# The first expert rows through a second DMA queue, and their squares on VectorE

## The chip, the cores and the metric

The kernel runs on one core of a Trainium2 chip. The core has five engines with programs of their own: TensorE multiplies matrices (PE in the profile, its weight loads are PEld), VectorE (DVE) and ScalarE (ACT) work on rows, GpSimd (POOL) does elementwise work beside them, and SyncE (SP) here only issues transfers. They meet through semaphores. The metric is the device time of one launch in microseconds; lower is better. The kernel before takes 1449.18 us (median of three runs, 1448.63 to 1451.13).

## The reference

For 2048 tokens of 576 features the result is `g * a + (1 - g) * b`, row by row:

```python
g = _sigmoid((x * gate_w).sum(-1, keepdims=True))
# a: a long convolution of each feature over time (state space model), by FFT, plus u * Dskip
# b: experts picked by product keys
q = jnp.einsum("nd,dhc->nhc", xf, w_q)               # 32 heads, two halves of 128
s1, s2 = scores of the halves against k1, k2          # 64 keys each
# best 2 of each, best 2 of the 4 sums, softmax -> gates g, expert numbers top_e
act = _gelu(jnp.einsum("nd,nhkd->nhk", xf, u[top_e]))
out = jnp.einsum("nhk,nhk,nhkd->nd", g, act, v[top_e])
```

The inputs that this change speaks of are the tokens `x` (the same array as the input of the convolution) and the expert rows `u`, 4096 rows of 576 features.

## The kernel before

The kernel does not gather the picked experts. It computes the products of all 2048 tokens with all 4096 expert rows (tile `a`), puts the gates at the picked places with one-hot products (tile `S`), and multiplies the resulting 2048 x 4096 weights with all rows of `v` (tile `o`). The scores are products of the folded query weights with the tokens (tile `s`). The convolution runs as matrix products in between. All large products are of 16-bit halves: a 32-bit operand is scaled by a power of two and split into a high and a low f16 part, and three products (high-high, high-low, low-high) are added up.

The power of two comes from the data. `scale_first` (line 500) does this for the two operands that are wanted first, the first 512 tokens and the first 512 expert rows: each is loaded as two halves of 256 features (tiles `xs` and `us`, 128 partitions by 2 by 512) and a rest of 64 features (`xr` and `ur`, stored twice, on both halves of the partitions); ScalarE squares the pieces and adds the squares of each partition into a column of `sc`; TensorE adds the columns over the partitions with a matrix of ones (tile `sq`); VectorE makes the scale from the sum (`root_scale`, line 346). Then the operand is split: for the tokens VectorE does both parts in `x_first` (line 478), for the expert rows ScalarE takes the high part and VectorE the low part in `u_build` (line 1323). The result tiles are `xb` and `uhl`, with `wrem` for the 64 features of the rest of the expert rows. The squares of the tokens are written into the tile `xb` of the next 512 tokens, and `x_norm` (line 460) multiplies them with ones on TensorE to get the norm of each token: for the first tokens it first runs eight such products whose result is overwritten, then waits until the expert scale is written, then runs the five that count.

The order of work is written by a planner inside the kernel's build. Pieces of work are Python generators; `clock` is TensorE's own time as the planner reckons it, each engine has a planned end time, and a generator that yields is taken up again when the planned clock has come so far. `dma` (line 200) issues a transfer and reckons with one wire and one queue when it lands. `ready(x)` yields until a tile is planned to be there. `marks` are lists by which the generators tell each other how far they are. The engines then run their programs strictly in the order in which the instructions were written; the planner's times decide only that order.

Transfers are issued on SyncE's queue, in the order of the program: the rest and the halves of the first tokens (`x_load`, line 430), the rest and the halves of the first expert rows (`u_load`, line 1309), the keys `kt`, the second 512 tokens, the query weights (`w_load`, line 565), the constants. The one use of ScalarE's queue is for half of the very last output rows (line 1628). The opening of the program is lines 1648 to 1655 for the transfers and 1687 to 1695 for the generators; lines 1703 to 1719 write the first 56 products `a`, in the order in which the split pieces come ready.

Of the kernel before, what the change touches and what calls it, by code (L numbers as in the profile page):

```python
# [17 lines left out]
AF = mybir.ActivationFunctionType  # L18
OP = mybir.AluOpType
# [119 lines left out]
def body(ctx: ExitStack, tc: tile.TileContext, xT, au, par, logdt, dskip, gatew, wq, kT, uT, vv,  # L139
         cst_d, tu_d, tk_d, tf_d, out):  # L140
    nc = tc.nc
# [3 lines left out]
    clock = [0.0]  # L145
    heap = []
    nseq = [0]
    rdy = {}
    table = [None]
    banks = set()  # L150
    wire = [0.0]
    queue = [0.0]
    tiling = [None]

    columns = set()
# [1 line left out]
    def key(x):  # L157
        n = x.tensor.name
        return (n, x.offset) if n in columns else n

    def size(x):
        n = 1
        for d in x.shape[1:]:
            n *= d
        return n
# [30 lines left out]
    S = Engine(nc.scalar, rdy, clock, key, act_cost)  # L196
    V = Engine(nc.vector, rdy, clock, key, dve_cost)
    G = Engine(nc.gpsimd, rdy, clock, key, lambda op, o, a, k: 0.15 + 0.0021 * size(o))

    def dma(o, i, q=None):  # L200
        t = max(clock[0], rdy.get(key(i), 0.0), queue[0])
        queue[0] = t + 0.45
        wire[0] = max(wire[0], t) + (2 if o.dtype in (F16, BF16) else 4) * o.shape[0] * size(o) / 3.4e5
        rdy[key(o)] = max(rdy.get(key(o), 0.0), wire[0] + 2.2)
        (q or DQ).dma_start(o, i)

    def mm(o, l, r, start, stop, cost=None):
        m = l.shape[0] > 64, 128 if size(l) > 64 else size(l)
        if m != tiling[0]:
            tiling[0] = m  # L210
            clock[0] += 0.13 if m == (True, 128) else 0.1
        clock[0] += (size(r) * (4 if r.dtype == F32 else 1) / 2400 + 0.003) if cost is None else cost
        rdy[key(o)] = clock[0] + 0.4
        T.matmul(o, l, r, start=start, stop=stop)  # L214
# [20 lines left out]
    def ready(*xs, late=0.0):  # L235
        while True:
            t = max(rdy.get(key(x), 0.0) for x in xs) + late - clock[0]
            if t <= 0:
                return
            yield t  # L240
# [20 lines left out]
    def need(tag, n=1):  # L261
        while True:
            lst = sorted(slots[tag])
            if len(lst) >= n and lst[n - 1] <= clock[0]:
                return
            yield max(0.2, lst[n - 1] - clock[0]) if len(lst) >= n else 0.3
# [6 lines left out]
    def free(tag, *outs):  # L273
        if owed[tag]:
            owed[tag] -= 1
            return
        slots[tag].append(max([clock[0]] + [rdy.get(key(x), 0.0) for x in outs]))
# [12 lines left out]
    def bank(tag, name):  # L290
        take(tag, name)
        t = ps.tile([128, 512], F32, tag="ps", name=name, bufs=8)
        banks.add(t.tensor.name)
        return t
# [7 lines left out]
    def row(x, name, pool):  # L302
        t = pool.tile([128, D], F32, name=name)
        dma(t, bass.AP(tensor=x.tensor, offset=x.offset, ap=[[0, 128], [1, D]]))
        return t
# [7 lines left out]
    def au_load(a, t):  # L313
        for d, o in au_rows(au, t, a):
            dma(o, d)
# [15 lines left out]
    sc = cp.tile([128, 192], F32, name="sc")  # L331
# [4 lines left out]
    def newcol(again=False):  # L336

        col[again] += 1
        c = 96 + col[1] % 96 if again else col[0]
        return slice(c, c + 1)  # L340

    def short(c0, n):

        return sc[:, c0:c0 + n].bitcast(BF16)[:, 1:2 * n:2]

    def root_scale(bound2, margin, again=False):

        c, h, a, b = (newcol(again) for _ in range(4))
        V.tensor_scalar(sc[:, c], bound2, margin, 2.0 ** -120, op0=OP.mult, op1=OP.max)
        V.tensor_scalar(sci[:, h], sc[:, c].bitcast(I32), 24, 23, op0=OP.logical_shift_right, op1=OP.logical_shift_left)  # L350
        V.tensor_scalar(sci[:, a], sci[:, h], -1.0, float(204 << 23), op0=OP.mult, op1=OP.add)
        V.tensor_scalar(sci[:, b], sci[:, h], float(50 << 23), None, op0=OP.add)
        return sci[:, a].bitcast(F32), sci[:, b].bitcast(F32)
# [32 lines left out]
    def slot(shape, dt, name):  # L386
        take("slot", name)
        return bp.tile([128] + shape, dt, tag="s", name=name, bufs=9)
# [32 lines left out]
    idx = wj.tile([128, NT, 64, 2], F16, name="idx")  # L421
    xb = []

    def halves_load(a, src, c):

        columns.add(a.tensor.name)
        for m in (0, 2):
            dma(a[:, m:m + 2], src[128 * m:128 * m + 256, c].rearrange("(k p) n -> p k n", p=128))

    def x_load(tb):  # L430
        a = slot([4, 512], F32, f"xs{tb}")
        r = pl.tile([128, 512], F32, tag="xr", name=f"xr{tb}", bufs=2)
        c = slice(512 * tb, 512 * tb + 512)
        if tb > 0:
            dma(a, xT[0:512, c].rearrange("(k p) n -> p k n", p=128))
        dma(r[0:64], xT[512:576, c])
        dma(r[64:128], xT[512:576, c])
        if tb == 0:
            halves_load(a, xT, c)
        return a, r  # L440

    def squares(a, r, sq, dst):
# [10 lines left out]
        V.tensor_reduce(out=dst, in_=p[:, 0:2], axis=AX, op=OP.add)  # L453
        free(tag, dst)

    marks = {"x": [], "s": [], "h": [], "u": []}
    first_u = [None, None]
    ahead, normed = [], []

# [18 lines left out]
    def x_first():  # L478

        a, r = xl.pop(0)  # L480
        b = slot([9, 512], F16, "xb0")
        first_u[1] = b
        ahead.append(slot([9, 512], F16, "xb1"))
        sq = ahead[0][:, 0:5].bitcast(BF16)
        s, i = yield from scale_first(a, r, sq)
        spawn(x_norm(0, sq))
        V.tensor_copy(i_x[:, 0:1], i)
        for k in range(5):
            while k == 2 and not marks["s"]:
                yield 0.1  # L490
            o, lo, src = (b[:, k], b[:, 4 + k], a[:, k, :]) if k < 4 else (b[:, 8], b[64:128, 8], r)
            p = slice(0, 128) if k < 4 else slice(64, 128)
            V.tensor_scalar(o, src, s, None, op0=OP.mult)
            V.scalar_tensor_tensor(lo, src[p], s[p], o[p], op0=OP.mult, op1=OP.subtract)
            marks["x"].append(V.free + 0.28)
        scaled.append(0)
        free("slot", b)
        xb.append(b)

    def scale_first(a, r, sq, keep=None):  # L500

        acc = [newcol() for _ in range(3)]
        yield from ready(r)
        S.activation(sq[:, 4], r, AF.Square, accum_out=sc[:, acc[0]])
        for n, m in enumerate((0, 2)):
            yield from ready(a[:, m:m + 2])
            S.activation(sq[:, m:m + 2], a[:, m:m + 2], AF.Square, accum_out=sc[:, acc[n + 1]])
        yield from ready(sq)
        yield from need("kb")
        p = bank("kb", "sq")  # L510
        for n in range(3):
            mm(p[:, 0:1], onesb, short(acc[n].start, 1), n == 0, n == 2, 0.05)
        yield from ready(p)
        out = root_scale(p[:, 0:1], 1.02)
        if keep is not None:
            V.tensor_copy(keep, p[:, 0:1])
        free("kb", out[0])
        return out

    def x_build(tb):  # L520
        while tb - 1 not in scaled:
            yield 0.3
        if tb not in xl:
            yield from need("slot", 2)
            xl[tb] = x_load(tb)
# [783 lines left out]
    def u_load(c):  # L1309
        a = slot([4, 512], F32, f"us{c}")  # L1310
        r = actp.tile([128, 512], F32, tag="ur", name=f"ur{c}")
        cs = slice(512 * c, 512 * c + 512)
        if c:
            dma(a, uT[0:512, cs].rearrange("(k p) n -> p k n", p=128))
        dma(r[0:64], uT[512:576, cs])
        dma(r[64:128], uT[512:576, cs])
        if c == 0:
            halves_load(a, uT, cs)
        return a, r

    uhl, i_u = {}, {}
# [1 line left out]
    def u_build(c):  # L1323
        while adone[0] < c - (kdone[0] < NCK or sdone[0] >= 7):
            yield 0.3
        if c:
            yield from need("raw")
            take("raw", "raw")
            yield from need("slot")
        a, r = xl.pop("u") if c == 0 else u_load(c)  # L1330
        if c:
            yield from ready(a, r)
# [3 lines left out]
        if c == 0:  # L1336
            first_u[0] = hl
            s, i = yield from scale_first(a, r, sq, nu[:, 0:1])
            marks["s"].append(1)
        else:  # L1340
            yield from squares(a, r, sq, nu[:, c:c + 1])
            s, i = root_scale(nu[:, c:c + 1], 1.02)
# [289 lines left out]
    def finish(t, po):  # L1632
# [7 lines left out]
        for d, o in au_rows(out, t, a):  # L1640
# [5 lines left out]
    acts = [(c, tb, j) for c, tb in [(c, tb) for c in range(7) for tb in range(4 if c < 6 else 2)] + [(7, 0), (7, 3), (6, 2), (6, 3), (7, 1), (7, 2)]  # L1646
            for j in range(4)]
    xl = {0: x_load(0)}
    take("raw", "raw")
    xl["u"] = u_load(0)  # L1650
    dma(kt, kT)
    xl[1] = x_load(1)
    w_load(0, 0)
    w_load(0, 1)
# [55 lines left out]
    for w, n in ((0, 9), (1, 5)):  # L1710
        for xk in [x for k in range(4) for x in (k, 4 + k)[:2 - w]] + [8]:
            k = 4 if xk == 8 else xk % 4
            landed("x", k)
            landed("hu"[w], k)
            for j in range(4):
                cs = slice(128 * j, 128 * j + 128)
# [8 lines left out]
    while groups or acts:  # L1725
# [5 lines left out]
        if groups and bank_free() and lag < (6.0 if not a_ok else 2.0 if not turn_s else 5.0 if kdone[0] < NCK else 8.0):  # L1731
            c, t = groups[0]
# [9 lines left out]
        if acts and bank_free():  # L1742
            c, tb, j = acts[0]
# [31 lines left out]
    for t in ORDER:  # L1775
        until(lambda: t in st)
        h = st.pop(t)
# [70 lines left out]
```

## Time and profile before

| what | us |
|---|---|
| median of 3 runs | 1449.18 (1448.63 to 1451.13) |
| profiled execution, from first to last instruction (its span) | 1447.6 |
| TensorE busy | 1426.9 |
| VectorE busy | 1208.5 |
| ScalarE busy | 769.6 |
| GpSimd busy | 481.5 |
| first ones-product of the long run on TensorE | at 9.37 |
| first product `a` | at 15.06 |

The profiled execution has no time of its own beside its span; the median of the runs is 1.6 us above it. A row of the timeline gives the start, the length, the engine, the line, the operation, the written tile, the tiles read and the shapes; in brackets is how long the engine sat idle before it and for what. Nearly all instructions carry the line of a helper (134 for VectorE, ScalarE and GpSimd, 205 for transfers, 214 for matrix products), so they are told apart by their tiles. A window's row gives busy time by engine, with the number of instructions in brackets, then the granted TensorE clock as a share of the full one, the busy share of the 16 DMA engines, and GB/s.

### The profile page before, as it was taken

The page shows a single profiled execution, that of the slowest core. Times are in us where ns is not written, and L with a number is a line of the kernel's source. Part 1 is how long each engine was busy: PE and PEld are TensorE (multiplying, and loading weights), DVE is VectorE, ACT ScalarE, POOL GpSimd, SP SyncE. Part 2 cuts the span into 40 slices and gives each one's busy share as a digit, 9 for nine tenths or more (in the row PEclk, how much of TensorE's full clock was granted, in tenths as well). Part 3 has the DMA queues.
Part 4 walks back from the last instruction along what each step waited for, and adds up shares of the span by engine and source line. Part 5 has one row for each costly group of instructions (what it writes and reads, how often), then busy time and mean ns, then how long its engine had stood idle before and what let it go on. Part 6 is the DMA issues. An engine that isn't in the chain of part 4 may idle for free.

```text
span 1447.6 us, 36680 instructions
## 1 busy us (share of the span) xinstructions
PE 1426.9 (99%) x14105; PEld 852.3 (59%) x14105; DVE 1208.5 (83%) x4598; ACT 769.6 (53%) x1285; POOL 481.5 (33%) x491
## 2 busy tenths in 40 slices
PE   7999999999999999999999999999999999999998
PEld 3444445455455445445555444456887887888787
DVE  6899899889877997885899897589999988888850
ACT  6346876796684776844656655655434223323310
POOL 0325357547356436220547899600000000000000
PEclk9999999999999999999999999999999999999999
DMA  8235323342324333169675777776543333342400
GB/s 308 74 117 159 96 74 120 125 143 72 117 93 150 95 105 99 49 199 293 209 272 179 255 256 270 267 259 210 196 127 111 108 120 107 123 145 68 157 10 17
DMA packets 134351, 215.42 MB, mean 149 GB/s; under 512 B 10912, under 2 KB 79904, under 8 KB 127776
## 3 DMA queue, kind: packets, MB, share of 16 engines
q1 hardware_dynamic: 134080, 213.01, 45.5%
q8 instruction: 110, 1.80, 0.5%
q14 instruction: 65, 0.53, 0.1%
q10 hardware_dynamic: 96, 0.07, 0.0%
HBM read 141.74 MB, written 71.30 MB: 147 GB/s over the span
## 4 chain that ended last, share of the span: by engine, by line
PE 89%; DMA 2%; DVE 2%; issue 0%; ACT 0%; SPq 0%; ACTq 0%; DVEq 0%
PE o L214 26%; PE s L214 24%; PE a L214 23%; PE S L214 4%; PE kb L214 2%; PE pr L214 2%; PE wb L214 2%; PE y L214 1%; PE kP L214 1%; PE pv L214 1%; PE u L214 1%; PE k L214 1%; DMA z_d<-vo 1%; DMA ksb<-k_d 1%; DVE i L134 1%; DMA vn<-in_au_dram 0%
## 5 line engine op out<-in xcount | busy, mean ns | idle before, releaser
L214 PE MATMUL o<-vhl,wh 128*128 128x288 f16 x3072 | 387.0, 286 | 0.0
L214 PE MATMUL s<-whl,xb 128*128 128x512 f16 x1536 | 363.9, 379 | 0.0
L214 PE MATMUL a<-xb,uhl 128*128 128x512 f16 x1536 | 359.7, 379 | 0.2 <-DVE go L134 0.2
L214 PEld LDWEIGHTS <-wh 128*128 128x128 f16 x3072 | 296.0, 98 | 76.3 <-issue 3.7
L214 PEld LDWEIGHTS <-xb 128*128 128x128 f16 x1792 | 170.6, 98 | 210.1 <-issue 15.3
L214 PEld LDWEIGHTS <-uhl 128*128 128x128 f16 x1536 | 147.3, 98 | 176.2 <-issue 3.4
L134 DVE FIND_INDEX8 i<-m,s 128x8 uint32<-128x64 f32 x1024 | 206.5, 222 | 0.0
L134 ACT ACTIVATE wh<-gl,s_wg 128x1024 f16<-128x1024 f32 x64 | 68.9, 1137 | 202.3 <-DVE gl L134 202.3
L134 DVE MAX8 m<-s 128x8 f32<-128x64 f32 x1024 | 146.3, 215 | 29.3 <-PE s L214 28.4
L134 POOL TENSOR_TENSOR CS<-CS,ex 128x512 f32<-128x512 f32 x72 | 98.0, 1393 | 147.6 <-DVE ex L134 146.2
L134 ACT ACTIVATE go<-a,i_a 128x512 f32<-128x512 f32 x94 | 63.2, 685 | 96.4 <-PE a L214 68.6
L134 DVE TENSOR_TENSOR gl<-S,gl 128x256 f32<-128x256 f32 x256 | 90.5, 416 | 12.6 <-PE S L214 8.3
L134 POOL TENSOR_TENSOR e<-aN,rt 128x512 f32<-128x512 f32 x72 | 83.2, 1177 | 49.9 <-PE kb L214 43.7
L134 DVE SCALAR_TENSOR_TENSOR wh<-gl,s_wg,wh 128x1024 f16<-128x1024 f32 x63 | 78.6, 1280 | 10.7 <-ACT wh L134 10.7
L134 DVE TENSOR_TENSOR Bg<-Be,vals 128x1024 f16<-128x1024 f16 x128 | 84.6, 702 | 2.2
L134 ACT ACTIVATE gl<-gl 128x1024 f32<-128x1024 f32 x64 | 63.5, 1045 | 34.2 <-DMA gl<-g_d 31.1
L134 DVE TENSOR_TENSOR A<-iota_a,vals 128x2048 f16<-128x2048 f16 x64 | 77.9, 1216 | 0.0
L214 PE MATMUL s<-wrem,xb 128*128 128x512 f16 x256 | 76.2, 379 | 0.0
L214 PE MATMUL a<-xb,wrem 128*128 128x512 f16 x256 | 75.9, 379 | 0.0
L214 PEld LDWEIGHTS <-A 128*128 128x128 f16 x2048 | 70.5, 97 | 4.7
L134 DVE MATCH_VALUE_LOAD i<-m,s 128x8 f32 x1024 | 72.6, 71 | 0.1
L214 PE MATMUL S<-Bg,A 128*128 128x64 f16 x2048 | 72.3, 193 | 0.0
(205 smaller groups left out, 2068.5 us busy)
## 6 DMA issues: line engine op xcount, KB each, us to landing
g_d<-go SPq DMA_DIRECT2D x128, 256.0 KB, 2.5
gl<-g_d SPq DMA_DIRECT2D x32, 1024.0 KB, 5.4
wq<-in_wq_dram SPq DMA_DIRECT2D x16, 1152.0 KB, 6.0
su_d<-us SPq DMA_DIRECT2D x32, 288.0 KB, 2.6
sk_d<-k1o SPq DMA_DIRECT2D x32, 288.0 KB, 2.9
ui<-su_d SPq DMA_DIRECT2D x16, 576.0 KB, 4.0
ki<-sk_d SPq DMA_DIRECT2D x16, 576.0 KB, 5.3
vn<-in_vv_dram SPq DMA_DIRECT2D x32, 288.0 KB, 5.4
```

The lines of the kernel that those rows point to most:

```text
L134: return f(*a, **k)
L214: T.matmul(o, l, r, start=start, stop=stop)
```

## The change

Four things change.

1. `halves_load` becomes `first_load`: for the first tokens and the first expert rows it issues the two halves first and the two copies of the rest behind them (before, the rest came first). It takes a queue.
2. The four transfers of the first expert rows go through ScalarE's queue (`nc.scalar`); the planner now reckons with one queue for each engine that issues.
3. In `scale_first` the pieces are squared in the order half, half, rest. For the expert rows the squares and their sums are made by VectorE (`tensor_tensor_reduce`) and no longer by ScalarE.
4. A new mark, `q`: the generator of the tokens writes its sum, and all that follows, only once the generator of the expert rows has written its squares.

```diff
     def dma(o, i, q=None):
-        t = max(clock[0], rdy.get(key(i), 0.0), queue[0])
-        queue[0] = t + 0.45
+        t = max(clock[0], rdy.get(key(i), 0.0), queues.get(id(q), 0.0))
+        queues[id(q)] = t + 0.45
...
-    def halves_load(a, src, c):
+    def first_load(a, r, src, q=None):
 
         columns.add(a.tensor.name)
         for m in (0, 2):
-            dma(a[:, m:m + 2], src[128 * m:128 * m + 256, c].rearrange("(k p) n -> p k n", p=128))
+            dma(a[:, m:m + 2], src[128 * m:128 * m + 256, 0:512].rearrange("(k p) n -> p k n", p=128), q)
+        for m in (0, 64):
+            dma(r[m:m + 64], src[512:576, 0:512], q)
...
-        if tb > 0:
-            dma(a, xT[0:512, c].rearrange("(k p) n -> p k n", p=128))
+        if tb == 0:
+            first_load(a, r, xT)
+            return a, r
+        dma(a, xT[0:512, c].rearrange("(k p) n -> p k n", p=128))
...
-    marks = {"x": [], "s": [], "h": [], "u": []}
+    marks = {"x": [], "s": [], "h": [], "u": [], "q": []}
...
     def scale_first(a, r, sq, keep=None):
 
         acc = [newcol() for _ in range(3)]
-        yield from ready(r)
-        S.activation(sq[:, 4], r, AF.Square, accum_out=sc[:, acc[0]])
-        for n, m in enumerate((0, 2)):
-            yield from ready(a[:, m:m + 2])
-            S.activation(sq[:, m:m + 2], a[:, m:m + 2], AF.Square, accum_out=sc[:, acc[n + 1]])
+        for n, (o, x) in enumerate(((sq[:, 0:2], a[:, 0:2]), (sq[:, 2:4], a[:, 2:4]), (sq[:, 4], r))):
+            yield from ready(x)
+            if keep is None:
+                S.activation(o, x, AF.Square, accum_out=sc[:, acc[n]])
+            else:
+                V.tensor_tensor_reduce(out=o, in0=x, in1=x, scale=1.0, scalar=0.0, op0=OP.mult, op1=OP.add,
+                                       accum_out=sc[:, acc[n]])
+        if keep is not None:
+            marks["q"].append(1)
+        while not marks["q"]:
+            yield 0.1
         yield from ready(sq)
...
-        if c:
-            dma(a, uT[0:512, cs].rearrange("(k p) n -> p k n", p=128))
+        if c == 0:
+            first_load(a, r, uT, nc.scalar)
+            return a, r
+        dma(a, uT[0:512, cs].rearrange("(k p) n -> p k n", p=128))
```

More of the change, by code (lines that the diff above doesn't have):

```diff
@@ L151, in body @@
     wire = [0.0]
-    queue = [0.0]
+    queues = {}
     tiling = [None]
@@ L433, in x_load @@
         c = slice(512 * tb, 512 * tb + 512)
-        if tb > 0:
-            dma(a, xT[0:512, c].rearrange("(k p) n -> p k n", p=128))
+        if tb == 0:
+            first_load(a, r, xT)
+            return a, r
+        dma(a, xT[0:512, c].rearrange("(k p) n -> p k n", p=128))
         dma(r[0:64], xT[512:576, c])
         dma(r[64:128], xT[512:576, c])
-        if tb == 0:
-            halves_load(a, xT, c)
         return a, r
@@ L1312, in u_load @@
         cs = slice(512 * c, 512 * c + 512)
-        if c:
-            dma(a, uT[0:512, cs].rearrange("(k p) n -> p k n", p=128))
+        if c == 0:
+            first_load(a, r, uT, nc.scalar)
+            return a, r
+        dma(a, uT[0:512, cs].rearrange("(k p) n -> p k n", p=128))
         dma(r[0:64], uT[512:576, cs])
         dma(r[64:128], uT[512:576, cs])
-        if c == 0:
-            halves_load(a, uT, cs)
         return a, r
```

## The prediction

> **What bounds the kernel now.** I read the page's busy times first, then the busy time by stretch, with edges where the start of the program changes character (columns: stretch, its length, then busy us and number of instructions of PE, PEld, DVE, ACT and POOL, the granted clock, the DMA share and GB/s).
>
> ```profile
> PE 1426.9 (99%) x14105; PEld 852.3 (59%) x14105; DVE 1208.5 (83%) x4598; ACT 769.6 (53%) x1285; POOL 481.5 (33%) x491
> ```
>
> ```profile
> core 0 of [0], span 1447.6 us
> 0.00:9.37 9.37, 0.35 (x4) 0.34 (x4) 1.00 (x6) 4.58 (x9) 0.20 (x4) 1.00 0.73 222
> 9.37:15.06 5.69, 5.69 (x17) 2.04 (x17) 4.78 (x17) 4.11 (x9) 0.00 (x0) 1.00 1.08 363
> 15.06:31.00 15.94, 15.86 (x137) 8.29 (x136) 12.81 (x28) 12.30 (x20) 0.00 (x0) 1.00 1.02 387
> 31.00:1443.97 1412.97, 1405.04 (x13950) 841.60 (x13949) 1189.43 (x4549) 748.56 (x1251) 481.31 (x487) 1.00 0.45 145
> 1443.97:1447.57 3.60, 0.00 (x0) 0.00 (x0) 0.52 (x1) 0.00 (x0) 0.00 (x0) 1.00 0.15 41
> ```
>
> TensorE is the bound: of 20.6 us in which it is idle, 9.0 lie before 9.37 us, 3.6 behind its last matmul, and 7.9 (1412.97 - 1405.04) are scattered between 31 us and the end. The change touches only the start. So whatever moves the first product of the expert rows (tile `a`) moves all the rest with it, unless the scattered idle time changes. The start on TensorE, ScalarE and VectorE, in order of time:
>
> ```profile
> 4.95 0.16 PE L214 MATMUL sq<-sc,onesb 128*128 128x1 bf16 x1 [4.95 <-ACT xb L134]
> 7.58 0.16 PE L214 MATMUL sq<-sc,onesb 128*128 128x1 bf16 x1 [2.47 <-ACT xb L134]
> 9.34 0.16 PE L214 MATMUL sq<-sc,onesb 128*128 128x1 bf16 x1 [1.60 <-ACT xb L134]
> 9.37 3.57 PE L214 MATMUL x<-xb,onesb 128*128 128x512 bf16 x8
> 12.74 0.38 PE L214 MATMUL sq<-sc,onesb 128*128 128x1 bf16 x3
> 12.97 2.29 PE L214 MATMUL x<-xb,onesb 128*128 128x512 bf16 x5
> 15.06 2.84 PE L214 MATMUL a<-xb,uhl 128*128 128x512 f16 x12
> ```
>
> ```profile
> 0.73 1.28 ACT L134 ACT_TABLE_LOAD   x1 [0.73 <-PEq L1838]
> ...
> 4.18 0.63 ACT L134 ACTIVATE xb<-xr 128x512 bf16<-128x512 f32 x1 [1.95 <-DMA xr<-in_xT_dram]
> ...
> 8.14 1.06 ACT L134 ACTIVATE xb<-xs 128x1024 bf16<-128x1024 f32 x1 [0.61 <-DMA xs<-in_xT_dram]
> ...
> 11.75 1.06 ACT L134 ACTIVATE uhl<-us 128x1024 bf16<-128x1024 f32 x1 [0.22 <-DMA us<-in_uT_dram]
> ...
> 17.06 1.89 ACT L134 ACTIVATE xb<-xs 128x2048 bf16<-128x2048 f32 x1
> ```
>
> ```profile
> 9.54 0.16 DVE L134 TENSOR_SCALAR sc<-sq 128x1 f32<-128x1 f32 x1 [7.59 <-PE sq L214]
> ...
> 11.94 0.75 DVE L134 SCALAR_TENSOR_TENSOR xb<-xs,sci,xb 128x512 f16<-128x512 f32 x1
> 13.15 0.16 DVE L134 TENSOR_SCALAR sc<-sq 128x1 f32<-128x1 f32 x1 [0.46 <-PE sq L214]
> ```
>
> The reader is to see a rigid block. The last token rows land at 8.1 us; ScalarE squares them, and 1.20 us after it began (8.14 to 9.34) TensorE adds the squares up. From there TensorE doesn't stop: 8 ones-matmuls, the 3 sums of the expert rows, 5 more ones-matmuls, and `a` at 15.06, 5.72 us after 9.34. The expert rows land at 11.75 and are squared inside this block, at no cost of their own. The start is set by when the **token** rows have landed and are squared; the expert rows come just in time.
>
> **The change part by part.** First the loads. Now one queue issues all of them:
>
> ```profile
> 0.73 1.23 SPq L205 DMA_DIRECT2D xr<-in_xT_dram  x2
> 2.01 1.09 SPq L205 DMA_DIRECT2D xs<-in_xT_dram  x2
> 3.15 1.12 SPq L205 DMA_DIRECT2D ur<-in_uT_dram  x2
> 4.30 1.10 SPq L205 DMA_DIRECT2D us<-in_uT_dram  x2
> ```
>
> After the change the tokens' four transfers go from 0.73 us on SyncE's queue, the large halves ahead of the 64-row rest, and the four of the expert rows at the same time on ScalarE's queue. Each set is 1.31 MB (1.05 in the halves, twice 0.131 in the rest), 2.62 MB together. What the wire moves at the start:
>
> ```profile
> 2.10:3.40 1.30, 0.00 (x0) 0.00 (x0) 0.00 (x0) 0.13 (x1) 0.00 (x0) 1.00 0.74 206
> 3.40:5.50 2.10, 0.16 (x1) 0.10 (x1) 0.00 (x0) 0.72 (x2) 0.00 (x0) 1.00 0.85 218
> 5.50:7.50 2.00, 0.00 (x0) 0.00 (x0) 0.00 (x0) 1.12 (x2) 0.00 (x0) 1.00 1.06 390
> ```
>
> By the stretches, 2.08 MB (9.37 us at 222 GB/s) have moved by 9.37, and 2.62 MB by 10.86 (0.54 MB more at 363 GB/s). The last expert half lands 0.9 us later (11.75). Two queues move the same bytes over the same wire; the tokens no longer have it to themselves, so with equal shares both sets end together, where now only the expert rows end. Bounds for the tokens' landing, X: not later than 11.75, as now; with equal shares not earlier than 2.1 + 6.8 (2.62 MB at 387 GB/s) + 0.9 = 9.8. Between them: the wire is starved from 2.1 to 3.4 because small transfers were issued first, and that goes. But from 3.4 to 5.5 over a megabyte is queued, and it runs at 218 all the same, with the engines 85% busy. So I take a good half of the starved 1.3 us as saved: X = 11.0.
>
> The Trainium skill's page "DMA: Bandwidth & Descriptors", section "Issuing engines are not separate DMA queues", speaks against this edit: transfers started from several engines run on the same 16 DMA engines and interleave, and only the issuing time is saved. By the rule alone X would be near 11.7, by the rate of 390 GB/s alone 9.8; the trace, with busy shares from 0.85 up on one queue, leans to the rule.
>
> Next the squares. The rest of the token rows comes last now, so ScalarE's last square is the 128x512 one: 0.77 us from its start to TensorE's sum (4.18 to 4.95) in place of 1.20, a gain of 0.43. The sum for `a` is X + 0.77 + 5.72 = 17.5 us with X = 11.0, against 15.06: **+2.4 us**. The bounds of X give 16.3 (+1.2) and 18.2 (+3.2).
>
> VectorE's squares, three new instructions, aren't in the trace; the nearest row is a two-input operation of its own:
>
> ```profile
> L134 DVE SCALAR_TENSOR_TENSOR wh<-gl,s_wg,wh 128x1024 f16<-128x1024 f32 x63 | 78.6, 1280 | 10.7 <-ACT wh L134 10.7
> ```
>
> So 1.28 us for a half and 0.75 (the row at 11.94) for the rest; as bounds, half of that and twice that. Two of the three lie under the remaining transfers. The third stands ahead of the tokens' scale in VectorE's order: by the new mark the token generator writes its sum, its scale and the first two splits only once the expert squares are written. From that scale to the end of the second split takes 3.15 us (9.54 to 12.69), from the expert scale to `a` 1.91 (13.15 to 15.06). So a second floor for `a` is U + 0.75 + 3.15 + 1.91 = U + 5.8, U being the landing of the expert rows: 16.8 with U = 11.0, 0.7 under the other floor. It costs nothing while U isn't over 0.7 us later than X. It also closes the way out by unequal shares: were the tokens served first and X still 8.1, U would be 11.75 and `a` at 17.5 again; with the wire full as well, U = 9.8 and `a` at 15.6 (+0.5), the lowest that the loads allow.
>
> The expert squares leave ScalarE (two of 1.06, one of about 0.63, and their reads). That is worth nothing: the last of them ends at 12.8, when TensorE's eight ones-matmuls are just done (12.74 to 12.94); those are the cover, and without it at most the 0.1 us between would show. ScalarE takes on four issues, at SyncE's 0.55 to 0.6 us each, ahead of its table load: 0.73 + 2.4 + 1.28 + 0.2 puts its first square at 4.6 us at the earliest, before any 512 KB half can land (today the 128 KB pieces alone take until 4.18): nothing. On SyncE's queue everything behind (keys, next tokens, query weights) moves up by 2.2 us; ScalarE took the next tokens' squares at 17.06 without a wait for them, so nothing is gained there.
>
> Sum: +2.4 us. The profiled execution's span is 1447.6, 1.6 below the median of the runs, and I take that 1.6 as unchanged: 1449.2 + 2.4 = **1451.6 us**.
>
> **The rivals.**
>
> *Expert rows late, VectorE as the new bound.* If ScalarE issues its loads only after the table load (ends at 2.01), they start 1.3 us late; SyncE's queue, done with the tokens, goes on to keys and next tokens, which take their share from the expert rows. The 0.27 MB moved before them (1.3 us at 206) are then extra: 2.9 MB, at 363 GB/s 0.7 us more, U = 11.6 + 0.9 = 12.5, and `a` at U + 5.8 = 18.3. If another half's square is still to do then, 1.28 more: 19.6. It decides from U over X + 0.7. That is +3.2 to +4.5, say +3.9: 1453.1. For it: VectorE's order is written so. Against: the loads stand first in ScalarE's program.
>
> *The slow matmuls end at a fixed time.* The ones-matmuls take 0.43 us each (12.74 less 9.37, by 8), those of `a` 0.23 (12 in 2.84), though the granted clock reads 1.00 in both stretches; the pace changes at about 15.06. If that moment stays while the block starts at 11.8, seven or eight of 13 run slow and the others at 0.22, `a` could start at 16.7, and VectorE's floor holds it at 16.8: +1.7, 1450.9. If it comes 5.7 us after the block's start, as here, nothing changes. The Trainium skill, "TensorE: Matmul & The Clock Gate", section "Part 1: The HAM clock gate (the "warmup" mystery)", says that the window which ends the half rate runs freely, apart from the kernel's start; one trace can't show this.
>
> *Two queues fill the wire from the first byte.* X = 9.8: `a` at 16.3, +1.2, 1450.4. The 390 GB/s behind 5.5 us speak for it, the 218 of 3.4 to 5.5 with enough queued against.
>
> *Faster.* The planner writes every later instruction by its own clock, and the new chain moves that. What can be gained there is bounded by the waits of TensorE behind 31 us; the longest:
>
> ```profile
> PE sq L214 <- ACT uhl L134: 1.8, 1, 1.8
> PE k L214 <- ACT k1o L134: 1.5, 1, 1.5
> PE kb L214 <- issue: 1.5, 1, 1.5
> PE u L214 <- DVE uh L134: 1.4, 1, 1.4
> ```
>
> With all four gone, 1451.6 - 6.2 = 1445.4. A shuffled order can as well add such waits, so this is a long shot.
>
> **How the numbers follow.** Forecast 0.42 (its own range 1450.2 to 1453.0), VectorE as bound 0.25, fixed clock 0.15, full wire 0.10, faster 0.08. A measurement of this kernel tells about 0.2% (2.9 us) from no change, so slower begins at 1452.1: nearly all of the VectorE case, a third of the forecast's and a little of the others make 0.39; faster 0.09; within 0.52. The range takes in the full wire and the VectorE case, with two to three microseconds of shuffled waits on either side: 1447.5 to 1455.0.
>
> **What would show it.** Right: the last token square starts on ScalarE at 10.5 to 11.7 in place of 8.14, the first `a` at 16.8 to 18.2, TensorE's block starts at 11 to 12.5 us, and behind it some 7.9 us of scattered idle time remain. VectorE case: TensorE waits in front of the expert sums or of `a`, with VectorE busy from the last expert square without a gap. Full wire: over 350 GB/s from 2.5 us. Wrong altogether: the tokens land by 8.5 us although the expert rows share the wire, or the scattered idle time changes by more than 3 us.

## The result, and the profile after

The changed kernel takes 1465.49 us (median of six runs, 1464.88 to 1470.87), the kernel before beside it 1449.83 (six runs, 1448.13 to 1453.28). The ratio is 1.0109 (95%: 1.0096 to 1.0121): slower by about 15.8 us, where 1451.6 was forecast and 1455.0 was the upper end of the range. The profiled executions are 1463.1 and 1447.6 us long, 15.5 apart.

First the busy times of the page of the changed kernel, then its time by stretch, with edges at 9.37 us and at the events of the prediction (start of the ones-matmuls, first `a`, 15.9 us later, last matmul):

```profile
PE 1431.4 (98%) x14105; PEld 853.7 (58%) x14105; DVE 1206.5 (82%) x4596; ACT 772.6 (53%) x1287; POOL 481.3 (33%) x492
```

```profile
core 0 of [0], span 1463.1 us
...
0.00:9.37 9.37, 0.16 (x1) 0.21 (x2) 2.23 (x8) 2.64 (x4) 0.20 (x4) 1.00 0.77 250
9.37:12.52 3.15, 0.19 (x3) 0.13 (x3) 1.64 (x3) 1.87 (x4) 0.00 (x0) 1.00 1.07 286
12.52:17.58 5.06, 4.90 (x18) 1.70 (x17) 4.42 (x18) 0.78 (x2) 0.00 (x0) 1.00 1.06 349
17.58:33.50 15.92, 15.82 (x136) 8.26 (x137) 13.31 (x29) 12.67 (x20) 0.00 (x0) 1.00 0.90 336
33.50:1459.50 1426.00, 1410.36 (x13950) 843.36 (x13949) 1184.39 (x4542) 754.65 (x1259) 481.11 (x488) 1.00 0.45 144
1459.50:1463.10 3.60, 0.00 (x0) 0.00 (x0) 0.51 (x1) 0.00 (x0) 0.00 (x0) 1.00 0.15 41
```

Set beside the rows of before, the first `a` comes at 17.58 in place of 15.06: +2.5 us, the predicted +2.4. In the 15.9 us behind it TensorE does as many products as before (136 against 137, 0.10 us idle against 0.08), and the end behind the last matmul is 3.6 us as it was. The rest of the loss, 13.0 us, lies in the long stretch with the same 13,950 matmuls: 1426.00 us in place of 1412.97. In it TensorE is idle 15.64 us in place of 7.93 (+7.7), and busy 1410.36 in place of 1405.04 (+5.3). So a change of eight transfers and six squares at the start costs five times as much behind the start as where it was made.

The opening in the timeline of the changed kernel:

```profile
0.74 1.03 ACTq L205 DMA_DIRECT2D us<-in_uT_dram  x2
...
1.80 1.43 ACTq L205 DMA_DIRECT2D ur<-in_uT_dram  x2
3.26 1.28 ACT L134 ACT_TABLE_LOAD   x1 [3.26 <-issue]
...
6.55 1.23 DVE L134 CUSTOM_DVE_ANT_0 uhl<-us 128x1024 bf16<-128x1024 f32 x1 [4.59 <-DMA us<-in_uT_dram]
...
11.72 0.63 ACT L134 ACTIVATE xb<-xr 128x512 bf16<-128x512 f32 x1 [0.95 <-DMA xr<-in_xT_dram]
12.11 0.69 DVE L134 CUSTOM_DVE_ANT_0 uhl<-ur 128x512 bf16<-128x512 f32 x1 [0.37 <-DMA ur<-in_uT_dram]
...
12.49 0.16 PE L214 MATMUL sq<-sc,onesb 128*128 128x1 bf16 x1 [1.51 <-ACT xb L134]
12.52 3.58 PE L214 MATMUL x<-xb,onesb 128*128 128x512 bf16 x8
...
16.01 1.40 PE L214 MATMUL x<-xb,onesb 128*128 128x512 bf16 x5
...
17.58 2.76 PE L214 MATMUL a<-xb,uhl 128*128 128x512 f16 x12 [0.16 <-ACT uhl L134]
```

Both sets end together, tokens at 11.72 and expert rows at 12.11 (the starts of the last squares, which waited for the transfers), and the block on TensorE follows the tokens. The squares on VectorE took 1.23 and 0.69 us. Now the long stretch in parts, of the kernel before and of the changed one:

```profile
31.00:500.00 469.00, 464.23 (x4249) 229.44 (x4249) 411.48 (x1741) 316.14 (x474) 231.66 (x186) 1.00 0.36 111
500.00:1000.00 500.00, 496.88 (x4618) 253.68 (x4617) 416.62 (x2218) 298.77 (x643) 247.35 (x301) 1.00 0.62 206
1000.00:1100.00 100.00, 100.00 (x1198) 80.30 (x1197) 97.44 (x157) 39.96 (x43) 2.30 (x1) 1.00 0.48 154
1100.00:1443.97 343.97, 343.94 (x3891) 278.18 (x3889) 263.89 (x436) 93.69 (x94) 0.00 (x0) 1.00 0.31 101
```

```profile
33.50:500.00 466.50, 460.60 (x4107) 226.92 (x4107) 394.53 (x1727) 316.44 (x474) 226.65 (x181) 1.00 0.36 108
500.00:1000.00 500.00, 495.14 (x4667) 251.26 (x4666) 420.53 (x2206) 304.42 (x649) 251.42 (x307) 1.00 0.63 208
1000.00:1100.00 100.00, 95.17 (x1106) 75.11 (x1103) 90.33 (x153) 35.18 (x37) 3.03 (x1) 0.97 0.49 156
1100.00:1459.50 359.50, 359.45 (x4081) 290.07 (x4078) 279.01 (x460) 98.62 (x100) 0.00 (x0) 1.00 0.31 97
```

The idle time (length less the first busy figure) is 4.77, 3.12, 0.00 and 0.03 us before, and 5.90, 4.86, 4.83 and 0.05 after. The largest piece, 4.8 us, lies between 1000 and 1100 us, where TensorE had not waited at all, and where the granted clock is now 0.97. What TensorE waited for:

```profile
PE S L214 <- DVE Bg L134: 4.8, 4, 3.2
...
PE wn L214 <- DVE i L134: 2.1, 2, 1.2
PE a L214 <- DVE i L134: 1.8, 1, 1.8
...
PE kb L214 <- POOL CS L134: 1.5, 2, 0.9
```

None of these four is among the eight waits that the same view shows of the kernel before. They are new waits, because the order is new. In the two built programs TensorE's weight loads and matmuls are the same, with the running numbers of the buffers left out; up to the 149th matmul they stand in the same order, and of all 20,962 some 4,000 stand at another place. So do some 500 of VectorE's 3,574 instructions and 400 of ScalarE's 1,187, the change's own among them. The planner's own clock behind the first 56 products (a number inside the build, no time of the chip) stands at 30.49 before and 32.02 after, and pieces of work that are taken up by that clock come in another order.

The longest new wait in the timeline, and around it the granted clock (the figure behind the five engines):

```profile
1012.69 5.15 SPq L205 DMA_DIRECT2D ya<-in_au_dram  x8
...
1017.88 0.90 SPq L205 DMA_DIRECT2D gl<-g_d  x2
...
1023.79 2.01 ACT L134 ACTIVATE gl<-gl 128x1024 f32<-128x1024 f32 x2 [9.64 <-DMA gl<-g_d]
...
1029.33 1.28 DVE L134 SCALAR_TENSOR_TENSOR wh<-gl,s_wg,wh 128x1024 f16<-128x1024 f32 x1 [4.34 <-ACT wh L134]
...
1034.46 0.24 PE L214 MATMUL S<-Bg,A 128*128 128x64 f16 x1 [3.18 <-DVE Bg L134]
```

```profile
1030.00:1032.00 2.00, 1.28 (x11) 0.78 (x8) 2.00 (x6) 0.63 (x1) 0.00 (x0) 1.00 0.62 166
1032.00:1034.00 2.00, 0.00 (x0) 0.00 (x0) 1.97 (x3) 0.00 (x0) 0.00 (x0) 0.89 0.76 151
1034.00:1036.00 2.00, 1.18 (x20) 1.08 (x21) 2.00 (x6) 0.00 (x0) 0.00 (x0) 0.50 0.84 324
1036.00:1038.00 2.00, 2.00 (x23) 1.53 (x21) 2.00 (x3) 0.00 (x0) 0.00 (x0) 0.50 1.02 430
1038.00:1040.00 2.00, 2.00 (x10) 1.19 (x9) 1.97 (x6) 0.00 (x0) 0.00 (x0) 0.50 0.55 229
```

The reader is to see a wait that is paid twice. The loads `gl` stand behind eight loads `ya` in SyncE's queue; ScalarE idles 9.64 us for them, VectorE 4.34 for ScalarE, TensorE 3.18 for VectorE. Then the granted clock falls to 0.50 for six microseconds, in which TensorE is busy 5.2 us and does the work of half of that. So idling costs 3.5 us here, and another 2.6 or so (an estimate from the granted clock) come back as busy time: half of the +5.3. The other half isn't tied to a cause.

### The profile page after: what moved, and what is told of

Same layout as the page of the kernel before. It is cut to its first block, busy times and chain, and to the rows that moved or that the text cites. A ratio compares the mean times of both kernels' runs of the same rounds, so it can differ in the third digit from the quotient of the medians.

```text
span 1463.1 us, 36672 instructions
## 1 busy us (share of the span) xinstructions
PE 1431.4 (98%) x14105; PEld 853.7 (58%) x14105; DVE 1206.5 (82%) x4596; ACT 772.6 (53%) x1287; POOL 481.3 (33%) x492
## 4 chain that ended last, share of the span: by engine, by line
PE 89%; DVE 5%; DMA 2%; ACT 1%; issue 1%; SPq 1%; DVEq 0%; ACTq 0%
PE o L214 25%; PE a L214 24%; PE s L214 23%; PE S L214 4%; PE pr L214 2%; PE wb L214 2%; PE kb L214 2%; PE y L214 1%; PE pv L214 1%; DVE i L134 1%; PE k L214 1%; PE kP L214 1%; PE u L214 1%; DMA wq<-in_wq_dram 1%; DVE m L134 1%
## 5 line engine op out<-in xcount | busy, mean ns | idle before, releaser
L214 PEld LDWEIGHTS <-xb 128*128 128x128 f16 x1792 | 170.7, 98 | 207.5 <-issue 13.9
L134 ACT ACTIVATE go<-a,i_a 128x512 f32<-128x512 f32 x85 | 57.5, 685 | 84.0 <-PE a L214 46.0
L134 DVE TENSOR_TENSOR gl<-S,gl 128x256 f32<-128x256 f32 x256 | 90.5, 417 | 10.5 <-PE S L214 6.7
L134 DVE MATCH_VALUE_LOAD i<-m,s 128x8 f32 x1024 | 77.0, 75 | 0.1
```

The lines of the kernel that those rows point to most:

```text
L134: return f(*a, **k)
```

## The experiments

Most of these kernels separate what the chip does at the start from the order that the planner writes behind it. For that, the planner goes on reckoning with one opening while another is emitted: `plan` reckons an instruction without issuing it, and `emit=False` does the same for a transfer.

**start_only**: the changed opening with the order of before. Its `first_load` issues the transfers without reckoning them.

```diff
-            dma(a[:, m:m + 2], src[...])
+            dma(a[:, m:m + 2], src[...], emit=False)
...
+            first_load(a, r, uT, nc.scalar)
...
-        S.activation(sq[:, 4], r, AF.Square, accum_out=sc[:, acc[0]])
+        S.plan("activation", sq[:, 4], r, AF.Square, accum_out=sc[:, acc[0]])
...
+                nc.vector.tensor_tensor_reduce(out=o, in0=x, in1=x, ...)
```

> The changed kernel's opening (loads on two queues, halves first, the expert squares on VectorE, ahead of the token scale) with the later order of the kernel before: on TensorE and GpSimd the order is that of before throughout, on VectorE, ScalarE and SyncE only the opening's own instructions differ. Theory A (the opening costs its 2.5 us and the other 13 us come from the order of the later work): first product a near 17.6, TensorE's scattered idle time behind 31 us near 7.9, time about 1452.3 (+2.5). Rival B (the new opening itself disturbs later work, by ScalarE's queue or by data that come at other times): 1458 or more, with new waits of TensorE behind 31 us.

**plan_only**: the opening of before with the changed order, by the same means the other way round.

```diff
-                S.activation(o, x, AF.Square, accum_out=sc[:, acc[n]])
+                S.plan("activation", o, x, AF.Square, accum_out=sc[:, acc[n]])
...
+            nc.scalar.activation(o, x, AF.Square, accum_out=sc[:, acc[n]])
```

> The reverse: the opening of the kernel before on the chip (one queue, rest first, all squares on ScalarE), the later order of the changed kernel. Theory A: first product a near 15.1, later waits as in the changed kernel (4.8 us on the one-hot tile Bg, clock 0.998), time about 1463.0 (2.5 under the changed kernel, 13 over the one before). Rival B: about 1450, as before.

In the built programs TensorE's and GpSimd's instructions stand in start_only exactly in the order of before, and in plan_only exactly in that of the changed kernel.

Measured: start_only 1453.96 us, ratio 1.0030 (1.0015 to 1.0044); plan_only 1464.79 us (four runs, 1461.80 to 1469.31), ratio 1.0096 (1.0079 to 1.0113). The order alone carries most of the loss, the opening alone a small one. In the timeline of start_only and of plan_only the first `a` stands where the opening puts it:

```profile
12.05 3.55 PE L222 MATMUL x<-xb,onesb 128*128 128x512 bf16 x8
...
17.09 2.76 PE L222 MATMUL a<-xb,uhl 128*128 128x512 f16 x12 [0.33 <-ACT uhl L134]
```

```profile
10.42 3.17 PE L222 MATMUL x<-xb,onesb 128*128 128x512 bf16 x8
...
15.24 2.76 PE L222 MATMUL a<-xb,uhl 128*128 128x512 f16 x12 [0.34 <-ACT uhl L134]
```

plan_only starts as early as the kernel before, to 0.2 us, and still ends as late as the changed one. Its waits:

```profile
PE S L222 <- DVE Bg L134: 5.4, 4, 3.8
PE wn L222 <- ACT wj L134: 5.3, 6, 1.2
...
PE a L222 <- DVE i L134: 1.8, 1, 1.8
```

The waits for `Bg` and for `i` are those of the changed kernel. By the 500th matmul, some 94 us in, plan_only already stands 2.7 us behind the kernel before and the changed kernel 3.0: what one has ahead at the start is gone by then. Part of it is a half clock that only plan_only's trace has there, 3.41 us from 84.7 on, behind a wait of 2.1 us.

**gl_act**: the changed kernel, with the loads `gl` of the stalled group through ScalarE's queue, past the `ya` loads and beside the `yz` loads that stand ahead of them.

```diff
-            dma(gl[h], g_d[t][:, 16 * h:16 * h + 16])
+            dma(gl[h], g_d[t][:, 16 * h:16 * h + 16], via=nc.scalar if t == ORDER[2] else None)
```

> The changed kernel, in which the two loads of the third group's products (tile gl, behind eight loads of ya in SyncE's queue) are issued by ScalarE's queue; the planner's reckoning and so every other order is unchanged. Theory A1 (the 3.2 us wait of TensorE near 1034 us and the half clock behind it come from these loads waiting in SyncE's queue): VectorE's wait of 4.3 us for the high part wh gone, clock 1.000, time about 1458.7 (6.8 less: 3.5 of idle time, 3.3 of slow clock). Rival (the loads wait for their buffers, not for the queue, or the wire is the limit): 1464 to 1466, the wait stays.

Measured: 1464.81 us, ratio 1.0112 (1.0092 to 1.0132): nothing is gained. The wait for `Bg` shrinks, and another takes its place:

```profile
PE y L214 <- DMA yz<-z_d: 3.5, 2, 3.3
...
PE S L214 <- DVE Bg L134: 1.3, 2, 0.9
```

ScalarE takes the first `gl` at 1017.12 in place of 1023.79, but the products `y` behind `yz` start at 1020.26 in place of 1016.89, and the clock is halved here too: between 1020 and 1040 us it is 0.91. The queue position was not the cause by itself: what `gl` gains, `yz` loses.

**loads_only**: the changed loads with all squares on ScalarE, order of before (start_only without its VectorE squares).

```diff
-                nc.vector.tensor_tensor_reduce(out=o, in0=x, in1=x, ...)
+                nc.scalar.activation(o, x, AF.Square, accum_out=sc[:, acc[n]])
```

> The kernel before with the changed loads alone (two queues, halves first; token pieces squared in the order half, half, rest); the expert squares stay on ScalarE behind the token squares, the later order is that of before. If the shared wire is the whole cost of the opening: last token square at 11.7 on ScalarE, the ones-products start near 12.5, a near 17.6, time about 1452.3 (+2.5). If VectorE's squares are part of the cost: a before 17.

Measured: 1453.02 us, ratio 1.0019 (1.0004 to 1.0035), first `a` at 18.21. The intervals of this and of start_only overlap, so the times can't tell the loads alone from the whole opening, and the place of the squares is lost in the spread. Its first `a` comes 1.1 us later than start_only's, but its last token square, whose loads are the same in both, already starts 0.9 us later.

The next four ask whether the changed order is bad for a reason of its own, or whether the order of before is a rare good one, so that any other would lose.

**nudge06** and **late27**: the kernel before, its opening untouched; the planner's clock is set ahead, by 0.6 us behind the first 56 products, or by 2.7 us in front of them.

```diff
     del acts[0:4]
+    clock[0] += 0.6
```

```diff
     first = [bank("sc", f"a0_0_{j}") for j in range(4)]
+    clock[0] += 2.7
```

> The kernel before, with nothing of the change; the planner's clock alone is set forward by 0.6 us once the first 56 products are written. The opening's instructions are those of before, the later order differs on every engine. Theory C (any small shift of the planner's clock gives another order, and orders differ by many microseconds): 1445 to 1466, not within 2 us of before in all four kernels of this set. Rival D (the order of the changed kernel is bad for a reason of its own, a shift alone does no harm): 1448 to 1453 here.

> The kernel before, with nothing of the change; the planner's clock alone is set forward by 2.7 us ahead of the first 56 products, which is about what the changed opening does to it. Theory C: another order, 1445 to 1466, with waits of TensorE behind 31 us that are not those of before. Rival D: 1448 to 1453. If the delay of the planner's clock by just this much is what makes the changed kernel's order bad: 1460 or more.

**after06**: the changed kernel, with the same 0.6 us behind the first products.

> The changed kernel, with the planner's clock set forward by 0.6 us more once the first 56 products are written; the opening is that of the changed kernel. Theory C: the 13 us are not a property of the change but of the one order it happened to get, so this one lies elsewhere, between 1448 and 1466, and the waits near 1004 and 1034 us on the one-hot tile are gone or moved. Rival D: 1463 to 1468, with the same waits.

**kp33**: the kernel before, with the parameters' generator taken up at 33 us of the planner's clock and not at 30.

```diff
-    spawn(k_params(), 30)
+    spawn(k_params(), 33)
```

> The kernel before, with nothing of the change; the planner takes up the parameters of the convolution at 33 us of its clock in place of 30 (their distance to the first products in the changed kernel's reckoning, reversed in sign). Theory C: another order, 1445 to 1466. Rival D: 1448 to 1453.

| kernel | us | ratio to before (95%) |
|---|---|---|
| nudge06 | 1480.99 | 1.0198 (1.0181 to 1.0215) |
| late27 | 1506.76 | 1.0379 (1.0357 to 1.0400) |
| kp33 | 1465.33 | 1.0101 (1.0084 to 1.0118) |
| after06 | 1455.00 | 1.0027 (1.0016 to 1.0037) |

Three reshufflings of the kernel before, none of which touches the data or the opening, cost 1.0 to 3.8%, two of them more than was expected of any. The same 0.6 us that ruin the kernel before take most of the loss off the changed one, because they bring its order back: of TensorE's 20,962 instructions ten stand in after06 at another place than before. Its 0.27% is that of start_only, 0.30%. Nor is a late clock of the planner what makes an order bad: behind the first 56 products it stands at 30.49 in the kernel before and at 32.62 in after06, with nearly the same order, and at 31.09, 32.02 and 32.47 in nudge06, the changed kernel and late27. (The changed opening moves it by 1.5 us there, not by the 2.7 that late27 was built for.) The waits of nudge06 show the same place as the costliest:

```profile
PE S L214 <- DVE Bg L134: 23.1, 10, 10.0
```

late27 spreads its waits over more places (7.8 us for an issue before `kb`, 7.4 for `wj`, 7.1 for `vhl`). In these traces the granted clock is halved for 34.1 us (nudge06) and 47.8 us (late27), in kp33 never behind the start, and its trace is 12.8 us longer all the same. So the size of the shift in planned time says nothing about its price: 0.6 us cost more than the change itself.

**squares_only**: only the expert squares go to VectorE; loads and order of before.

```diff
+                nc.vector.tensor_tensor_reduce(out=o, in0=x, in1=x, ...)
...
+        if keep is None:
+            for n, (o, x) in enumerate(pieces):
+                nc.scalar.activation(o, x, AF.Square, accum_out=sc[:, acc[n]])
```

> The kernel before with the expert squares alone moved: VectorE makes them, ahead of the token scale in its order; loads and later order are those of before. By the second floor of the prediction (VectorE's order): the last expert square is a half, starts when it lands at 11.75 and ends near 13.0, then 3.15 us from the token scale to the second split and 1.9 us from the expert scale: a at 18.1, with TensorE waiting in front of the expert scale or of a; time about 1453 (+3). If the squares on VectorE cost nothing: a at 15.1, time within 1 us of before.

Measured: 1457.32 us, ratio 1.0041 (1.0025 to 1.0058). The timeline shows the second floor of the prediction at work:

```profile
11.96 1.23 DVE L514 CUSTOM_DVE_ANT_0 uhl<-us 128x1024 bf16<-128x1024 f32 x1 [0.17 <-DMA us<-in_uT_dram]
...
13.11 0.15 DVE L134 TENSOR_SCALAR sc<-sq 128x1 f32<-128x1 f32 x1
...
16.17 0.15 DVE L134 TENSOR_SCALAR sc<-sq 128x1 f32<-128x1 f32 x1
```

```profile
17.51 3.73 PE L222 MATMUL a<-xb,uhl 128*128 128x512 f16 x9 [2.66 <-ACT uhl L134]
```

The tokens' sum was ready nearly as before (9.67 us against 9.34), but VectorE takes their scale only when the last expert square is done, at 13.11, and TensorE idles 2.66 us in front of `a`, which then runs slow (9 products in 3.73 us). Moving the squares without the loads costs 2.4 us up to the first `a`, and 4.0 by 24 us, behind the slow products. The trace is of the fastest of the five runs (1453.16 us); what the others lost beyond that, no trace shows.

**warm** and **warm2** try the other way: a faster start under the order of before. One queue carries the halves of the tokens, their rest, then the expert rows; all squares stay on ScalarE; and 80 small products, whose result is overwritten, keep TensorE busy until the tokens are there. warm2 adds 36 more of them in front of the expert sums (`else 36` in place of `else 0`).

```diff
+        for _ in range(80 if keep is None else 0):
+            T.matmul(p[:, 128:256], onesb, onesb, start=True, stop=True)
         for n in range(3):
             mm(p[:, 0:1], onesb, ...)
```

> A version after the findings, with the later order of before: one queue, the token pieces ahead of the expert pieces, halves ahead of the rests, all squares on ScalarE in that order, and 80 small products of ones ahead of the first sum (they fill the first 8 us of TensorE and are overwritten). If the ones-products run at the full rate behind them and the last square of each set is the short one: the block starts near 8.9, a at 14.2 to 14.6 in place of 15.06, time 0.5 to 0.8 us under before, which the times can hardly tell. If the slow pace doesn't end earlier: a near 14.7.

> The version before it (one queue, token pieces first, short squares last, 80 small products of ones at the front) with 36 more such products between the eight ones-products and the sums of the expert rows, where TensorE stood idle for 2.3 us and its clock fell to half for 3.4 us just as the products a began. If that idle time is what lowers the clock: the granted clock stays 1.00 from 14.15 to 18.3, the first 12 products a take 2.8 us in place of 4.3, a still begins near 14.2, time 1.5 us under that version and some 5 us under the kernel before. If the clock falls for another reason: 0.62 in that stretch again and the same time.

Measured: warm 1447.75 us (12 runs), ratio 0.9975 (0.9965 to 0.9985), a quarter of a per cent below the kernel before, where 0.5 to 0.8 us were expected; warm2 1448.45 us (11 runs), ratio 0.9988 (0.9977 to 0.9999). With the tokens first on one queue, their last square starts ahead of the kernel before (8.14) and far ahead of the changed kernel (11.72):

```profile
7.65 0.63 ACT L527 ACTIVATE xb<-xr 128x512 bf16<-128x512 f32 x1
```

So it was the second queue that made the tokens late, not the order of halves and rest. The stretch from the first `a`, in warm and then in warm2:

```profile
14.15:18.30 4.15, 4.15 (x12) 1.57 (x13) 4.05 (x7) 4.15 (x6) 0.00 (x0) 0.62 1.04 356
```

```profile
14.15:18.30 4.15, 4.15 (x21) 1.91 (x20) 4.05 (x8) 4.15 (x7) 0.00 (x0) 1.00 1.00 378
```

In warm TensorE had little to do between 10.2 and 12.6 us, and the clock is 0.62 in this stretch; the fillers of warm2 keep it at 1.00, and 21 products fit where 12 did. That mechanism is shown. The 1.5 us expected of it are not seen in the total: in the traces warm2 stands 1.1 us ahead of the kernel before behind its opening and 1.4 ahead at the end, warm 0.6 behind and 1.5 ahead. Which of the two is better these times can't tell, and the traces account for only part of warm's 0.25% (3.6 us).

## Why the prediction was wrong, step by step

- **TensorE bounds, and a later first `a` moves the rest with it.** Right in the changed kernel up to 33.5 us, and roughly in start_only: its `a` comes 2.0 us later (0.14%), the times say +0.30% (0.15 to 0.44). In its trace, of the fastest of six runs, it is still 2.0 us behind at 360 us and 0.6 at the end.
- **The sum for `a`, +2.4.** Right in its total (17.58 against 17.5) by luck: two errors cancel. The tokens landed at 11.72, not at 11.0. The starved stretch went (299 GB/s from 2.5 to 5.5 us), but the two sets didn't have the wire to themselves: by 12.2 us 3.13 MB had moved, where the sets are 2.62, since SyncE's queue had gone on to the keys (issued at 6.21) and the next tokens (6.60). The 0.77 us to TensorE's sum were exact (11.72 to 12.49). The block took 5.09 us, not 5.72, since its last five ones-matmuls ran fast (1.40 us in place of 2.29); why, is told under the slow matmuls.
- **The rule against the edit.** The Trainium skill, "DMA: Bandwidth & Descriptors", section "Issuing engines are not separate DMA queues", has transfers of several engines interleave on the same 16 DMA engines. The trace agrees: the tokens landed at 11.72, where the prediction put the rule's outcome, near 11.7. The second queue brought the expert rows no sooner (12.11 against 11.75).
- **The full wire** fell: 333 GB/s from 2.5 to 9.37 us (299 up to 5.5, 360 behind), where over 350 from 2.5 on was the sign.
- **VectorE as the new bound** did not decide in the changed kernel. ScalarE issued its loads before its table load. The last expert square came 0.39 us behind the last token square, inside the 0.7 that the prediction allowed, and VectorE still waited 0.36 us for TensorE in front of the expert scale. squares_only shows that the floor is real: `a` at 17.51, where the floor's formula, with the loads of before and a half as the last square, would give 18.1 (11.75 + 1.28 + 3.15 + 1.91). It was less because the ones-matmuls were done by 14.85, so that from the expert scale (16.17) `a` waited for its split alone: 1.34 us, not 1.91.
- **The costs of VectorE's squares** (1.28 and 0.75 expected, 1.23 and 0.69 measured), of the issues on ScalarE and of the move up on SyncE's queue were right and cost nothing on the path.
- **Slow matmuls that end at a fixed time.** Neither of the two readings held. Each trace keeps the changes of the granted clock, and its first record stands where the matmuls turn fast: at 15.23 us before, 16.37 in the changed kernel, 13.05 in plan_only and 15.45 in start_only. From the block's start that is 5.9, 3.9, 2.6 and 3.4 us, so the slow phase isn't tied to the block; nor is its end tied to the program's start. The 0.63 us that the block gained are therefore chance. That fits the free-running window of the Trainium skill, "TensorE: Matmul & The Clock Gate", section "Part 1: The HAM clock gate (the "warmup" mystery)". The trace agrees: in each of the 13 traces the changes of the granted clock lie whole multiples of 3.41 us apart, and where that grid stands against the start differs from trace to trace.
- **The step that failed** is the last one of the working: that the scattered idle time would stay, with "two to three microseconds of shuffled waits on either side". The prediction saw that the planner writes every later instruction by its own clock. It then bounded what this can gain by the waits of before (6.2 us), and took the loss to be about as small as a part of that. But the waits that exist bound only a gain. What an order can lose isn't bounded by them: the new waits stand at places where the kernel before had none. In the trace the stretch behind 33.5 us grew by 13.0 us: 7.7 of idle time, and 5.3 of busy time, about half of it work at half clock behind a wait. The prediction had a chance of 0.08 on the side of a gain and nothing on the side of a loss beyond 3 us, and no term for a clock that falls behind a wait. Of the two signs that it named as "wrong altogether" one came: the scattered idle time changed by more than 3 us.

The order and the opening, crossed:

| | order of before | changed order |
|---|---|---|
| opening of before | 1 | 1.0096 (plan_only) |
| changed opening | 1.0030 (start_only), 1.0027 (after06, 20 lines apart) | 1.0109 |

The loss is the opening's 0.3% plus the order's 1.0%, within the intervals. What stays open: why the order of before is so much better than its four neighbours (the changed order, nudge06, late27 and kp33). No run found a single cause. The stall at `S` was cured at one place (gl_act) and came back at another. That it's an order that was picked out among many is a guess from these four, not shown.

## What to carry to other kernels

Where a planner with its own clock writes the order of work, an edit at the start isn't local: price it as its local term plus a new draw of every later wait, and where the trace shows a bound engine with almost no waits (20.6 us of 1447.6 here), that draw can lose far more than it can gain: the four other orders here lost 1.0 to 3.8%, and all waits of before together are worth 7.9 us. Measure such an edit with the order held fixed, and cross the two (old and new edit by old and new order), before the edit itself is judged. A second queue doesn't speed up a load whose wire is already busy; here it only took the wire from the transfer that was wanted first (last token square at 11.72 us, against 7.65 in warm on one queue).

## What was not expected of the hardware

- A short idle of TensorE can cost twice, and its place decides. In all 13 traces the records of the granted clock stand on a grid of 3.41 us, and half clock lasts 3.41, 6.83, 10.24, 13.65 or 17.07 us. Adding up TensorE's idle time in each piece of that grid at full clock: behind all fourteen pieces with 2.07 us or more the clock was halved, behind none with 1.83 or less, and in between (1.89 to 2.03) behind two of four. So the 3.18 us in front of 1034.46 were paid twice, 2.27 of them lying in one piece; in warm 1.99 us of idle time between 10.5 and 13.9 us were followed by half clock from 13.92 to 17.34, over a microsecond after work had begun again (12.54), and 12 products took 4.32 us in place of 2.76. A longer wait in kp33, split by the grid into 1.20 and 2.03 us, was followed by no half clock:

```profile
84.15 0.16 PE L214 MATMUL sq<-sc,onesb 128*128 128x2 bf16 x1 [3.24 <-ACT uhl L134]
```

- The windows' rows read 1.00 for the clock from the first microsecond, though matmuls run at half pace for the first 3 to 6 us of work: ahead of a trace's first record (15.23 us before) the 1.00 stands for no record. In warm the 80 small products took 7.50 us from 1.05 on, the first record stands at 7.09, and the ones-matmuls behind them ran fast from the first (8 in 1.89 us in place of 3.57).
- VectorE's square with its sum, 128x1024, took 1.23 us, no more than an operation that reads two tensors and sums nothing (1.28), plus 0.08 us to read the sum.
